# The same linear attention and PReLU layer, its list of operations written out in another order

## The chip, the cores and the metric

The kernel runs on one core of a Trainium2 chip. The metric is device microseconds (us) of one execution. The core has five engines with an instruction queue each: TensorE (PE; PEld is its weight loads), VectorE (DVE), ScalarE (ACT), GpSimd (POOL) and SyncE (SP), which does nothing here but issue transfers. Every queue runs strictly in the order in which the program was written; an instruction that waits holds up all behind it on its engine, and nothing on the others.

## The reference

q, k and v are 4 batches x 8 heads x 768 positions x 64 (float32). Attention is linear with a decay per head: within a block, products of q and k are multiplied by powers of the head's lambda and applied to v; across blocks, a 64 x 64 state per head is decayed and added to. Its output, as 3072 tokens x 512, goes through a two-layer network.

```python
intra = einsum('bhij,bhjd->bhid', einsum('bhic,bhjc->bhij', qb, kb) * Dmask, vb)
inter = einsum('bhid,bhde->bhie', qb * lam_pow, kv_state)
kv_state = lam_block * kv_state + einsum('bhsd,bhse->bhde', kb * rev_pow, vb)
h = x @ w_in                                  # 512 x 2048
out = (maximum(h, 0) + alpha * minimum(h, 0)) @ w_out   # 2048 x 512
```

## The kernel before, in words

The tokens are taken in six chunks of 512 (two batches x 256 positions). A chunk has four attention units, so there are 24, numbered 0 to 23: unit n belongs to chunk n // 4, to batch half (n // 2) % 2 and to head half n % 2. For a unit the program writes these steps:

- `load` brings float32 keys or queries (512 KB for a batch half, by SP's queue or, with ring=1, by POOL's, L89); `load16` brings queries of the first chunks, and all values, cast to half precision on the way by POOL's queue (L102).
- `cast` (L248 ACT, L250 DVE, L252 POOL) copies keys or queries into one half-precision tile qk. `turn` (L291) transposes that tile on PE for units 0 to 7, and `turned` copies the result from PSUM to qkT; from unit 8 on `turn_by_dma` (L305) has SP issue a transposing transfer instead.
- `key_decayed` (L279) and `decayed` (L321) multiply keys and turned queries by powers of lambda.
- `cluster(old, new)` on PE finishes unit old (L344 with the state RD, L374 with the masked scores) and starts unit new (scores s at L362, key-value products at L391).
- `masked` (L403, DVE) multiplies the scores by the decay mask; `state` (L428 DVE, L425 ACT) updates the state; `spread` copies it into RD, where the next cluster reads it; `out_of` copies the unit's output to xT.

The network: `up` (L457) makes 128 rows of h from w_in for a whole chunk or one batch half, in a PSUM bank; `below` (L468, ACT) takes the negative part m; `gate` (L481, DVE) joins them to g, which frees the bank for a later `up`; `down` (L491) and, for chunks 3 to 5, `product` (L598) multiply g by w_out. w_in and w_out come in four pieces each by POOL's queue (`load_win` L110, `load_wout` L116).

At the start `fill` (L238) keeps PE busy with products of the identity that nobody reads; `slopes` (L229, L230) transposes alpha on PE and has DVE make oma from it; `decay_mask`, `key_decay` and `query_decay` are exponentials on ACT; `causal` zeroes the masks; `hold` writes one element of a key tile on DVE, so that the tile's load waits for DVE to reach that place. `warm_up` sets one element on DVE and takes its logarithm on ACT (L179), for which ACT loads a table of functions.

The order of all this is a list of 887 calls at the end of the function. The call order is the queue order of each engine; semaphores do the rest. Nothing is planned at run time.

Of the kernel before, what the change touches and what calls it, by code (L numbers as in the profile page):

```python
# [11 lines left out]
def kernel(  # L12
# [434 lines left out]
    G = {}  # L447
# [213 lines left out]
    zeros(1, 1)  # L661
    identity()
    load("k", 0, 0, 0)
    load_alpha()
    zeros(2, 1, "G")
    zeros(0, 0)
    load("q", 0, 0, 0)
    hold("k", 0, 1, 0)
    load16("q", 0, 0, 1)
    load("k", 0, 0, 1)  # L670
    load16("v", 0, 0, 0)
    fill(6, 2)
    fill(36, 2)
    hold("k", 1, 0)
    logs()
    key_decay(0)
    zeros(1, 0)
    cast(0, "k", "V")
    key_decay(1)
    zeros(0, 1)  # L680
    decay_mask(3, 1)
    cast(0, "q", "G")
    fill(16, 2)
    turn(0)
    load16("q", 0, 1)
    hold("k", 2, 0)
    cast(1, "k", "V")
    key_decayed(0, "V")
    query_decay(1)
    load("k", 0, 1, 1)  # L690
    decay_mask(2, 1)
    decay_mask(0, 0)
    fill(15, 2)
    cast(3, "k", "V")
    load16("v", 0, 0, 1)
    decay_mask(1, 0)
    load16("v", 0, 1)
    query_decay(2)
    turned(0, "A")
    key_decayed(1, "V")  # L700
    query_decay(0)
    cast(1, "q", "V")
    key_decayed(3, "V")
    load("k", 0, 1, 0)
    fill(5, 2)
    decay_mask(1, 1)
    state_decay()
    decay_mask(0, 1)
    turn(1)
    decayed(0, "V")  # L710
    cluster(None, 0)
    causal(0, 1)
    turned(1, "A")
    load_win(0)
    query_decay(3)
    load16("q", 1, 0)
    zeros(3, 0)
    spread(0, 1, "A", True)
    causal(0, 0)
    load16("v", 1, 0)  # L720
    decayed(1, "G")
    cast(2, "k", "V")
    masked(0, 1)
    fill(17)
    masked(0, 0)
    cast(2, "q", "A")
    state(0, 0)
    decay_mask(2, 0)
    decay_mask(3, 0)
    causal(1, 1, "G")  # L730
    load("k", 1, 0)
    turn(2)
    cluster(0, 1, True)
    cast(3, "q", "A")
    state(0, 1)
    causal(1, 0, "G")
    turned(2, "V")
    load_win(1)
    masked(1, 1)
    turn(3)  # L740
    state(1, 0)
    spread(1, 1, "A", True)
    masked(1, 0)
    out_of(0, "V")
    cluster(1, None)
    turned(3, "A")
    out_of(1, "A")
    slopes(2)
    key_decayed(2, "G")
    cluster(None, 2)  # L750
    masked(2, 0)
    state(1, 1)
    decayed(2, "G")
    spread(2, 1, "A", True)
    cast(4, "k", "G")
    load16("q", 1, 1)
    masked(2, 1)
    spread(9, 0, "A")
    state(2, 0)
    up(0, 0, 0, 2)  # L760
    cast(4, "q", "G")
    cluster(2, 3, True)
    state(2, 1)
    below(0, 0, 0)
    load_win(2)
    spread(3, 1, "A", True)
    decayed(3, "G")
    key_decayed(4, "G")
    state(3, 0)
    turn(4)  # L770
    gate(0, 0, 0)
    masked(3, 1)
    cast(5, "k", "G")
    up(0, 2, 0, 2)
    out_of(2, "A")
    below(0, 2, 0)
    cast(5, "q", "A")
    masked(3, 0)
    zeros(3, 1)
    gate(0, 2, 0)  # L780
    turned(4, "A")
    fill(14, 0)
    cluster(3, None)
    state(3, 1)
    up(0, 1, 0, 0)
    up(0, 3, 0, 2)
    out_of(3, "V")
    below(0, 1, 0)
    below(0, 3, 0)
    up(0, 6, None, 1)  # L790
    load_win(3)
    cast(6, "q", "G")
    gate(0, 1, 0)
    below(0, 6, None)
    key_decayed(5, "G")
    up(0, 2, 1, 0)
    gate(0, 3, 0)
    below(0, 2, 1)
    up(0, 5, None, 2)
    zeros(2, 0)  # L800
    hold("k", 1, 1)
    cluster(None, 4)
    gate(0, 2, 1)
    below(0, 5, None)
    decayed(4, "G")
    gate(0, 6, None)
    up(0, 0, 1, 0)
    cast(7, "q", "G")
    below(0, 0, 1)
    load16("v", 1, 1)  # L810
    gate(0, 5, None)
    masked(4, 1)
    up(0, 4, None, 1)
    gate(0, 0, 1)
    load_wout(1)
    up(0, 8, None, 2)
    below(0, 4, None)
    up(0, 3, 1, 0)
    load("k", 1, 1)
    gate(0, 4, None)  # L820
    below(0, 8, None)
    state(4, 0)
    below(0, 3, 1)
    gate(0, 8, None)
    load_wout(0)
    gate(0, 3, 1)
    turn(5)
    masked(4, 0)
    up(0, 7, None, 1)
    spread(4, 1, "G")  # L830
    turned(5, "A")
    below(0, 7, None)
    state(4, 1)
    up(0, 1, 1, 2)
    below(0, 1, 1)
    cast(6, "k", "G")
    gate(0, 7, None)
    key_decayed(6, "G")
    gate(0, 1, 1)
    spread(10, 0, "A")  # L840
    up(0, 9, None, 0)
    cluster(4, 5)
    up(0, 11, None, 2)
    below(0, 9, None)
    load_wout(2)
    turn(6)
    state(5, 0)
    up(0, 14, None, 1)
    decayed(5, "G")
    spread(5, 1, "G")  # L850
    masked(5, 0)
    state(5, 1)
    load("k", 2, 0, ring=1)
    masked(5, 1)
    below(0, 11, None)
    cast(7, "k", "G")
    gate(0, 9, None)
    up(0, 12, None, 0)
    gate(0, 11, None)
    load("q", 2, 0, ring=1)  # L860
    below(0, 14, None)
    out_of(4, "A")
    hold("k", 3, 0)
    below(0, 12, None)
    up(0, 10, None, 2)
    turned(6, "V")
    below(0, 10, None)
    key_decayed(7, "G")
    gate(0, 14, None)
    load16("v", 2, 0)  # L870
    gate(0, 12, None)
    cluster(5, None)
    up(0, 15, None, 1)
    out_of(5, "A")
    up(1, 0, 0, 0)
    below(1, 0, 0)
    below(0, 15, None)
    gate(0, 10, None)
    hold("k", 2, 1)
    up(0, 13, None, 2)  # L880
    below(0, 13, None)
    cluster(None, 6)
    load_wout(3)
    gate(1, 0, 0)
    gate(0, 15, None)
    gate(0, 13, None)
    state(6, 0)
    up(1, 2, 0, 0)
    below(1, 2, 0)
    masked(6, 1)  # L890
    gate(1, 2, 0)
    decayed(6, "V")
    state(6, 1)
    turn(7)
    down(0, 2, 0, 1)
    turned(7, "V")
    up(1, 1, 0, 2)
    load("k", 2, 1, ring=1)
    spread(11, 0, "V")
    spread(6, 1, "G")  # L900
    down(0, 2, 1, 2)
    spread(14, 0, "V")
    cast(8, "k", "A")
    down(0, 1, 0, 0)
    down(0, 1, 1, 2)
    masked(6, 0)
    down(0, 2, 2, 2)
    below(1, 1, 0)
    gate(1, 1, 0)
    key_decayed(8, "V")  # L910
    key_decayed(9, "G")
    cast(9, "k", "A")
    cast(8, "q", "G")
    cluster(6, 7)
    down(0, 0, 0, 2)
    down(0, 0, 1, 1)
    state(7, 0)
    turn_by_dma(8)
    decayed(7, "V")
    down(0, 0, 2, 1)  # L920
    spread(8, 0, "G")
    spread(7, 1, "A")
    cast(10, "k", "A")
    masked(7, 1)
    decayed(8, "G")
    cast(9, "q", "V")
    down(0, 1, 2, 2)
    down(0, 2, 3, 2)
    masked(7, 0)
    state(7, 1)  # L930
    out_of(6, "V")
    down(0, 0, 3, 1)
    cast(11, "k", "V")
    store(0, 0)
    store(0, 2)
    cluster(7, 8)
    load("q", 3, 1)
    down(0, 1, 3, 2)
    spread(13, 0, "V")
    load("k", 3, 1, ring=1)  # L940
    out_of(7, "V")
    state(8, 0)
    load("q", 3, 0, ring=1)
    up(1, 3, 0, 2)
    up(1, 4, None, 1)
    spread(8, 1, "G")
    key_decayed(11, "G")
    masked(8, 1)
    store(0, 1)
    below(1, 3, 0)  # L950
    masked(8, 0)
    state(8, 1)
    gate(1, 3, 0)
    load16("v", 2, 1)
    turn_by_dma(9)
    up(1, 5, None, 0)
    cast(14, "k", "G")
    decayed(9, "G")
    cast(14, "q", "G")
    below(1, 4, None)  # L960
    key_decayed(10, "G")
    cluster(8, 9)
    gate(1, 4, None)
    below(1, 5, None)
    up(1, 0, 1, 2)
    below(1, 0, 1)
    load("q", 2, 1)
    gate(1, 5, None)
    up(1, 1, 1, 1)
    state(9, 0)  # L970
    gate(1, 0, 1)
    below(1, 1, 1)
# [603 lines left out]
```

## Time and profile before

| | us |
|---|---|
| median of 3 runs | 214.76 (214.64 to 214.83) |
| the profiled execution's own time | 216.86 |
| its span, first to last instruction | 214.80 |
| PE busy in the span | 199.9 (93%) |
| DVE, ACT, POOL busy | 163.7, 109.4, 100.9 |
| read from and written to HBM | 27.28 MB, 6.29 MB |

In a row of the timeline stand the start, the length, the engine (q: its sequencer issues a transfer), the line, operation, out<-in with shapes, how many, and in brackets the idle time of the engine before it and what ended that. Rows that follow closely are merged. In a row of the table of stretches stand the stretch, its length, busy time of the engines with instructions in brackets, the granted TensorE clock, the busy share of the DMA engines (it can exceed 1, since overlapping packets count apart) and GB/s. TensorE's granted clock is 0.999 over the span.

### The profile page before, as it was taken

How to read it: one execution, taken by the hardware profiler on the slowest of the kernel's cores; microseconds unless marked ns; L12 is line 12 of the kernel's file. 1: busy time of each engine (PE TensorE's matmuls, PEld its weight loads, DVE VectorE, ACT ScalarE, POOL GpSimd, SP SyncE). 2: the span in 40 equal slices, each digit the busy share in tenths (PEclk: the TensorE clock that was granted, in tenths of full speed). 3: DMA queues.
4: the chain of work that ended last, by engine and by line, in shares of the span. 5: the costliest groups of instructions: out<-in, count | busy, mean ns of one | idle time of the engine just before them, and what ended most of it. 6: DMA issues, size and time to landing. Idle time of an engine off the chain costs nothing.

```text
span 214.8 us, 5663 instructions
## 1 busy us (share of the span) xinstructions
PE 199.9 (93%) x2286; PEld 124.1 (58%) x2286; DVE 163.7 (76%) x335; ACT 109.4 (51%) x219; POOL 100.9 (47%) x149
## 2 busy tenths in 40 slices
PE   4967899999999779999999989999999999999992
PEld 4955565655645345546454535556667756866881
DVE  3888699895959995599977948979785669478721
ACT  3988676542645512546764565327546334344320
POOL 7879788951829994990299265331040000000000
PEclk9999999999999999999999999999999999999999
DMA  4999999999999999999764299649223120102213
GB/s 122 270 194 195 195 212 202 252 226 229 323 240 200 217 224 236 231 189 252 151 119 80 76 217 149 173 123 192 56 99 53 52 98 2 49 25 76 70 56 121
DMA packets 59754, 33.54 MB, mean 156 GB/s; under 512 B 34496, under 2 KB 55504, under 8 KB 59728
## 3 DMA queue, kind: packets, MB, share of 16 engines
q0 software_dynamic: 22528, 14.03, 42.6%
q1 hardware_dynamic: 35296, 16.00, 34.0%
q10 hardware_dynamic: 1904, 3.16, 4.2%
q8 instruction: 18, 0.29, 0.5%
q14 instruction: 8, 0.07, 0.1%
HBM read 27.28 MB, written 6.29 MB: 156 GB/s over the span
## 4 chain that ended last, share of the span: by engine, by line
PE 72%; DMA 13%; POOL 6%; DVE 3%; issue 3%; ACT 1%; SPq 0%; DVEq 0%; ACTq 0%
PE h_ps L457 32%; PE p_ps L598 17%; PE o_ps L491 15%; DMA qraw<-in_q_dram 8%; DMA qh<-in_q_dram 5%; PE s L362 3%; PE acc L374 2%; PE acc L344 2%; POOL vh L102 2%; POOL qk L252 1%; DVE g L481 1%; POOL qdT L321 1%; PE acc L391 1%; DVE RD L250 1%; POOL RD L252 1%
## 5 line engine op out<-in xcount | busy, mean ns | idle before, releaser
L457 PE MATMUL h_ps<-xT,w_in_sb 128*128 128x512 f16 (+1 forms) x416 | 92.2, 363 | 3.3 <-DVE g L481 2.7
L481 DVE SCALAR_TENSOR_TENSOR g<-m,oma,h_ps 128x512 f16<-128x512 f32 (+1 forms) x104 | 71.5, 704 | 24.5 <-ACT m L468 23.0
L468 ACT ACTIVATE m<-h_ps 128x512 f32<-128x512 f32 (+1 forms) x104 | 57.1, 564 | 53.3 <-PE h_ps L457 50.0
L457 PEld LDWEIGHTS <-w_in_sb 128*128 128x128 f16 x416 | 39.2, 98 | 40.5 <-issue 3.2
L491 PE MATMUL o_ps<-w_out_sb,g 128*128 128x512 f16 x192 | 45.4, 379 | 0.0
L403 DVE TENSOR_TENSOR sm<-s,dmask 128x512 f16<-128x512 f32 x48 | 32.2, 685 | 2.7 <-PE s L362 2.5
L491 PEld LDWEIGHTS <-g 128*128 128x128 f16 x192 | 18.3, 98 | 20.8
L321 POOL TENSOR_TENSOR qdT<-qkT,qdecay 128x512 f16<-128x512 f16 (+1 forms) x19 | 19.8, 1045 | 5.9 <-DMA qkT<-qk 5.3
L598 PEld LDWEIGHTS <-g 128*128 128x128 f16 x192 | 18.7, 98 | 4.1
L279 POOL TENSOR_TENSOR kdec<-kraw,kdecay 128x512 f16<-128x512 f32 x17 | 18.1, 1064 | 5.1 <-PE acc L391 3.5
L252 POOL COPY RD<-R 64x128 f16<-64x128 f16 x34 | 12.1, 357 | 10.3 <-DVE R L428 9.3
L598 PEld LDWEIGHTS <-gsum 128*128 128x128 f16 x144 | 14.0, 98 | 3.4
L428 DVE SCALAR_TENSOR_TENSOR R<-R,rdecay,acc 128x64 f16<-128x64 f16 x60 | 14.0, 275 | 1.7 <-ACT R L425 0.8
L622 ACT ACTIVATE o_sb<-p_ps 128x512 f32<-128x512 f32 (+1 forms) x16 | 7.7, 489 | 13.6 <-PE p_ps L598 12.2
L511 ACT ACTIVATE o_sb<-o_ps 128x512 f32<-128x512 f32 x12 | 7.2, 597 | 12.5 <-PE o_ps L491 11.9
L252 POOL CAST qk<-qraw 128x512 f16<-128x512 f32 x12 | 7.3, 613 | 10.9 <-DMA qraw<-in_q_dram 10.8
L598 PE MATMUL p_ps<-wsum,gsum 128*128 128x256 f16 x96 | 12.0, 273 | 0.0
L598 PE MATMUL p_ps<-w_out_sb,g 128*128 128x256 f16 x96 | 11.9, 272 | 0.0
L248 ACT ACTIVATE xT<-acc 128x512 f16<-128x512 f32 x14 | 8.3, 595 | 6.8 <-DVE R L428 5.2
L598 PE MATMUL p_ps<-wsum,g 128*128 128x256 f16 x96 | 11.8, 273 | 0.0
L102 POOL DMA_DIRECT2D vh<-in_v_dram x13 | 11.7, 901 | 0.0
L238 PE MATMUL op_fill<-ident 128*128 128x128 f16 x109 | 8.8, 245 | 2.9 <-POOL ident masks.py:199 2.7
(88 smaller groups left out, 214.2 us busy)
## 6 DMA issues: line engine op xcount, KB each, us to landing
kraw<-in_k_dram SPq DMA_DIRECT2D x6, 512.0 KB, 8.7
out_dram<-o_sb ACTq DMA_DIRECT2D x12, 256.0 KB, 6.0
out_dram<-o_sb SPq DMA_DIRECT2D x24, 128.0 KB, 1.9
vh<-in_v_dram POOLq DMA_DIRECT2D x11, 256.0 KB, 8.0
qraw<-in_q_dram SPq DMA_DIRECT2D x5, 512.0 KB, 7.0
w_in_sb<-in_moe_w_in_dram POOLq DMA_DIRECT2D x4, 512.0 KB, 8.1
w_out_sb<-in_moe_w_out_dram POOLq DMA_DIRECT2D x4, 512.0 KB, 8.5
kraw<-in_k_dram POOLq DMA_DIRECT2D x4, 512.0 KB, 8.3
```

Source lines behind the costliest of these rows:

```text
L102: nc.gpsimd.dma_start(out=rows16(x, c, bi)[:, ds(h0, n), :], in_=source({"q": q, "v": v}[x], c, bi, h0, n))
L238: nc.tensor.matmul(t[:, 0:128], lhsT=ident, rhs=ident, start=True, stop=True)
L252: nc.gpsimd.tensor_copy(out=out, in_=in_)
L279: engine(eng).tensor_tensor(out=kdec, in0=kr, in1=d.unsqueeze(3).to_broadcast([128, 2, 4, D]), op=ALU.mult)
L321: engine(eng).tensor_tensor(out=x, in0=y, in1=d.unsqueeze(2).to_broadcast([128, 4, n, 64]), op=ALU.mult)
L403: nc.vector.tensor_tensor(out=t["sm"][hl], in0=t["s"][hl], in1=mask_of(hl, units[n][2]), op=ALU.mult)
L428: nc.vector.scalar_tensor_tensor(out=then[:, hp], in0=R[b, hh, i][:, hp], scalar=rdecay[:, 2 * hh + hp : 2 * hh + hp + 1], in1=kv[:, hp], ...
L457: nc.tensor.matmul(h_ps[:, 0:n] if bi is None else h_ps[:, 0:n].rearrange("p (e j) -> p e j", e=2), lhsT=w_in_sb[:, gi, ts(f, 128)], rhs=x ...
L468: nc.scalar.activation(m[:, 0:n], HP[c, f, bi][:, 0:n], AF.Relu, scale=-1.0)
L481: nc.vector.scalar_tensor_tensor(out=g, in0=mv, scalar=oma[:, f : f + 1], in1=hv, op0=ALU.mult, op1=ALU.add)
L491: nc.tensor.matmul(O[c, t], lhsT=gated(c, f)[:, t // 2, t % 2, :], rhs=w_out_sb[:, f, :], start=(f == 0), stop=(f == NF - 1),)
L598: nc.tensor.matmul(acc, lhsT=lhsT, rhs=rhs, start=(first and j == 0), stop=(j == NJ - 1), skip_group_check=True,)
```

## The change

The 887 calls are written in another order, and 97 of them have another engine, transfer queue or PSUM bank. The number of calls of each kind, the fills' total of 109 among them, is the same, and PE's instructions are as many as before (4573). Nothing outside the list changes. Two lines of the difference:

```diff
-    load("k", 1, 0)
+    load("k", 1, 0, ring=1)
```

What stands where is better seen in the queues. The first place is POOL's queue at the start of the program, from the last copy of the identity on. qh and vh are queries and values in half precision, kraw and qraw keys and queries in float32; 4x128 is half a tile, 8x128 a whole one. Before:

```order
L161 CAST ident_142<-ident 16x16
L175 MEMSET RD_1_136 128x512
L102 DMA qh<-in_q_dram 128x4x128
L102 DMA vh<-in_v_dram 128x4x128
L252 CAST qk_240<-qraw 128x512
L102 DMA qh<-in_q_dram 128x8x128
L102 DMA vh<-in_v_dram 128x4x128
L102 DMA vh<-in_v_dram 128x8x128
L110 DMA w_in_sb<-in_moe_w_in_dram 128x4x512
L102 DMA qh<-in_q_dram 128x8x128
L102 DMA vh<-in_v_dram 128x8x128
```

And now:

```order
L161 CAST ident_142<-ident 16x16
L102 DMA qh<-in_q_dram 128x4x128
L89 DMA kraw<-in_k_dram 128x4x128
L102 DMA vh<-in_v_dram 128x4x128
L102 DMA vh<-in_v_dram 128x8x128
L102 DMA qh<-in_q_dram 128x8x128
L102 DMA vh<-in_v_dram 128x4x128
L89 DMA kraw<-in_k_dram 128x8x128
L110 DMA w_in_sb<-in_moe_w_in_dram 128x4x512
L279 TENSOR_TENSOR kdec<-kraw,kdecay 128x512
L102 DMA qh<-in_q_dram 128x8x128
```

Half of the first chunk's second keys and all of the second chunk's first keys (kraw 8x128) have come from SP's queue to POOL's, ahead of the first piece of w_in; the cast that waited for queries is gone from between the issues; a memset of RD now stands ahead of the identity instead of behind it.

The second place is DVE's and ACT's queues in the first chunk. On DVE, from the last copy of llp on, before:

```order
L192 COPY llp<-loglam 64x4
L175 MEMSET RD_0_133 128x256
L250 CAST qk_240<-kraw 128x512
L175 MEMSET RD_1_132 128x256
L85 MEMSET kraw 1x1
L250 CAST qk_276<-kraw 128x512
```

And now, with unit 0's tile called qk_234:

```order
L192 COPY llp<-loglam 64x4
L175 MEMSET RD_0_133 128x256
L250 CAST qk_234<-qraw 128x512
L230 TENSOR_SCALAR oma<-at_ps 128x16
L250 CAST qk_234<-kraw 128x512
L85 MEMSET kraw 1x1
```

oma, which stood far behind in the first chunk, now stands ahead of the cast of unit 0's keys; PE has 47 fills (36 + 5 + 6) ahead of the transpose that oma reads, and does that transpose before it turns unit 0. On ACT, from the first m on, now:

```order
L468 ACTIVATE m<-h_ps 128x256
L179 ACT_TABLE_LOAD
L179 ACTIVATE warm<-one 128x1
L425 ACTIVATE R_0_1_101<-acc 128x128
L248 ACTIVATE RD_1_134<-h_acc 64x2x64 x2
L425 ACTIVATE R_1_1_106<-h_acc 128x128
L248 ACTIVATE xT<-h_acc 128x4x64 x2
L468 ACTIVATE m<-h_ps 128x256
```

The table load and the logarithm of `warm_up` stood in the fourth chunk before, between two m. They now stand behind the first m and ahead of the state copies of units 2 and 3, unit 3's spread and unit 2's output copies.

The third place is chunk 2's transfers (units 8 to 11). On POOL, from `decayed(8)` on, now (before, this product was followed by loads of the fourth chunk's second keys and first queries):

```order
L321 TENSOR_TENSOR qdT<-qkT,qdecay 128x512
L102 DMA vh<-in_v_dram 128x8x128
L89 DMA qraw<-in_q_dram 128x8x128
L102 DMA vh<-in_v_dram 128x8x128
L89 DMA kraw<-in_k_dram 128x8x128
L252 CAST qk_1257<-qraw 128x512
L321 TENSOR_TENSOR qdT<-qkT,qdecay 128x512
```

On SP, from unit 8's transpose on, before:

```order
L305 DMA_TRANSPOSE qkT<-qk_1147 128x8x128
L89 DMA qraw<-in_q_dram 128x8x128
L305 DMA_TRANSPOSE qkT<-qk_1171 128x8x128
L89 DMA qraw<-in_q_dram 128x8x128
L305 DMA_TRANSPOSE qkT<-qk_1249 128x8x128
L89 DMA kraw<-in_k_dram 128x8x128
L305 DMA_TRANSPOSE qkT<-qk_1273 128x8x128
```

And now:

```order
L305 DMA_TRANSPOSE qkT<-qk_1233 128x8x128
L305 DMA_TRANSPOSE qkT<-qk_1143 128x8x128
L89 DMA qraw<-in_q_dram 128x8x128
L305 DMA_TRANSPOSE qkT<-qk_1255 128x8x128
L305 DMA_TRANSPOSE qkT<-qk_1257 128x8x128
L89 DMA qraw<-in_q_dram 128x8x128
L89 DMA kraw<-in_k_dram 128x8x128
```

The third chunk's second queries (for units 10 and 11) were SP's second qraw; they are now POOL's first qraw, behind a product that needs unit 8's transposed tile. The fourth chunk's first keys (kraw, for units 12 and 13) stood on SP ahead of unit 11's transpose; they now stand behind it and behind a load of queries. Further on the list differs in the same manner: who casts and copies, and what stands a few rows earlier or later. Three of the four pieces of w_out were issued ahead of the third chunk's first keys; now all four stand behind them.

More of the change, by code (lines that the diff above doesn't have):

```diff
@@ L697 @@
[L697 to L719, printed above, removed]
-    load16("v", 1, 0)
@@ L747 @@
[L747 to L755, printed above, removed]
-    load16("q", 1, 1)
[L757 to L765, printed above, removed]
+    load16("q", 0, 0, 1)
+    cast(0, "q", "V")
+    fill(5, 2)
+    fill(6, 2)
+    slopes(2)
+    load("k", 0, 1, 1, ring=1)
@@ L812 @@
+    gate(0, 0, 1)
+    masked(4, 0)
+    load("k", 1, 1)
+    below(0, 4, None)
+    load16("v", 1, 1)
+    up(0, 8, None, 2)
+    hold("k", 3, 0)
+    up(0, 3, 1, 0)
+    load_wout(0)
+    spread(4, 1, "A")
+    turn(5)
+    cast(6, "k", "G")
+    below(0, 3, 1)
+    below(0, 8, None)
+    gate(0, 4, None)
     masked(4, 1)
-    up(0, 4, None, 1)
-    gate(0, 0, 1)
+    gate(0, 3, 1)
+    turned(5, "A")
+    up(0, 7, None, 1)
     load_wout(1)
-    up(0, 8, None, 2)
-    below(0, 4, None)
-    up(0, 3, 1, 0)
@@ L838 @@
-    key_decayed(6, "G")
[L839 to L845, printed above, removed]
-    turn(6)
[L847 to L859, printed above, removed]
+    cluster(4, 5)
+    below(0, 9, None)
@@ L894 @@
[L894 to L913, printed above, removed]
-    cluster(6, 7)
-    down(0, 0, 0, 2)
+    down(0, 1, 1, 2)
```

1241 lines of the change are left out of this document (651 added, 590 removed).

## The prediction

> **What bounds the kernel now.** The page's busy times come first, with the DMA engines' share by fortieths of the span.
>
> ```profile
> PE 199.9 (93%) x2286; PEld 124.1 (58%) x2286; DVE 163.7 (76%) x335; ACT 109.4 (51%) x219; POOL 100.9 (47%) x149
> DMA  4999999999999999999764299649223120102213
> ```
>
> PE is busy for 93% of the span, and the change leaves its instructions as they are, so time can only come from PE's idle stretches and fills. The DMA engines are full from the second fortieth to the nineteenth, up to about 100 us: in that half a transfer that is issued later, or behind others, lands later. Next comes PE by stretches: the busy time, the granted clock and the DMA share.
>
> ```profile
> 0.00:24.00 24.00, 17.16 (x362) 1.00 1.28 195
> 68.00:80.00 12.00, 9.40 (x102) 1.00 1.26 233
> 103.00:108.00 5.00, 4.63 (x62) 1.00 0.75 188
> 125.00:131.00 6.00, 5.06 (x64) 1.00 0.99 170
> 131.00:211.00 80.00, 79.75 (x752) 1.00 0.34 88
> ```
>
> The clock is 1.00 throughout. From 131 us on PE loses a quarter of a microsecond in 80, so the last 80 us hold nothing to win, only something to lose. The losses lie in the head and in three short stretches. In the head, PE's timeline:
>
> ```profile
> 2.72 5.42 PE L238 MATMUL op_fill<-ident 128*128 128x128 f16 x58 [2.72 <-POOL ident masks.py:199]
> ...
> 18.48 0.61 PE L457 MATMUL h_ps<-xT,w_in_sb 128*128 128x256 f16 x4 [0.57 <-DMA w_in_sb<-in_moe_w_in_dram]
> ...
> 23.57 3.21 PE L457 MATMUL h_ps<-xT,w_in_sb 128*128 128x256 f16 x20
> ```
>
> Until 18.48 PE waits for keys, queries and attention's small copies; the first `up` then waits for w_in's first piece, and from 23.57 PE is full. The three short stretches are these, with the idle time in brackets:
>
> ```profile
> 75.56 0.60 PE L457 MATMUL h_ps<-xT,w_in_sb 128*128 128x256 f16 x4 [1.77 <-DVE g L481]
> ...
> 78.82 0.29 PE L344 MATMUL acc<-qdT,RD 128*128 128x128 f16 x2 [0.83 <-DVE RD L250]
> ```
>
> ```profile
> 107.09 0.29 PE L344 MATMUL acc<-qdT,RD 128*128 128x128 f16 x2 [0.37 <-POOL RD L252]
> ```
>
> ```profile
> 129.12 1.02 PE L457 MATMUL h_ps<-xT,w_in_sb 128*128 128x512 f16 x4 [0.94 <-DVE g L481]
> ```
>
> Together 1.77 + 0.83 + 0.37 + 0.94 = 3.9 us. Each has a cause that the new order touches. Behind 75.56 stands one copy on DVE, here between POOL's rows of the same time, and below them a copy of the same shape elsewhere:
>
> ```profile
> 72.21 1.18 POOL L321 TENSOR_TENSOR qdT<-qkT,qdecay 128x512 f16<-128x512 f16 x1
> 72.27 2.58 DVE L250 CAST qk<-kraw 128x512 f16<-128x512 f32 x1
> ```
>
> then POOL's next:
>
> ```profile
> 73.32 0.62 POOL L252 CAST qk<-qraw 128x512 f16<-128x512 f32 x1
> ```
>
> ```profile
> 48.29 0.41 DVE L250 CAST qk<-qraw 128x512 f16<-128x512 f32 x1
> ```
>
> The cast took 2.58 us instead of 0.41, while POOL went from one instruction to the next without a pause; the gate behind it on DVE, and PE behind that gate, lost most of the 2.17 us. The one at 129.12 is ACT's table load:
>
> ```profile
> 126.31 1.28 ACT L179 ACT_TABLE_LOAD   x1
> ```
>
> and the logarithm behind it:
>
> ```profile
> 127.60 0.20 ACT L179 ACTIVATE warm<-one 128x1 f32<-128x1 f32 x1
> ```
>
> That is 1.48 us between two m of a stretch in which PE's next bank hangs on them.
>
> **The change part by part.** *The keys in POOL's queue ahead of w_in: nothing.* The transfers ahead of w_in's first piece are the same set as before (SP's halves and the second chunk's first keys, POOL's queries and values), the DMA engines are full, and one set takes one time in either queue: I keep 18.4 us for its landing. The bounds are half a microsecond to either side. The cover is the backlog: the eight issues ahead of the kdec take some 0.9 us each and the transfers longer.
>
> *The head: +1.0.* oma now waits for 47 fills, ahead of the cast of unit 0's keys.
>
> ```profile
> 2.85 0.51 POOL L175 MEMSET RD<- 128x512 f16 x1
> ```
>
> ```profile
> 5.61 0.43 DVE L250 CAST qk<-kraw 128x512 f16<-128x512 f32 x1
> ```
>
> and next on DVE but for fills of memory:
>
> ```profile
> 6.99 0.82 DVE L250 CAST qk<-kraw 128x512 f16<-128x512 f32 x1 [0.68 <-DMA kraw<-in_k_dram]
> ```
>
> ```profile
> 10.00:15.00 5.00, 3.49 (x114) 2.88 (x112) 4.27 (x12) 4.31 (x12) 3.84 (x5) 1.00 1.66 208
> 15.00:20.00 5.00, 3.65 (x116) 2.84 (x115) 4.33 (x13) 4.08 (x13) 4.64 (x7) 1.00 1.58 191
> ```
>
> The identity is 0.51 us later, since a memset of this length moves ahead of it; 47 fills at 5.42 / 58 = 0.093 us take 4.4 us; so DVE, which has the first cast done at about 6.0, stands until 2.72 + 0.51 + 4.4 = 7.6, or 7.9 with the hand-over. That is 1.9 us of standing in place of 0.68. DVE is then busy for 8.60 of the 10 us from 10 to 20 (third busy time in the rows), so 1.4 us of pauses can take up some of the 1.2 us; but PE's clusters run in turn with DVE's masks, and little of a pause that waits for PE can be used. On ACT, 1.28 + 0.20 = 1.48 us now stand ahead of unit 2's output copies, whose bank a fill and the next `up` need; ACT has 8.39 of 10 us filled there. The two delays overlap. The head costs nothing if the pauses take up all, and 1.2 + 1.48 = 2.7 us if none: I take 1.0, near the single delays.
>
> *The second chunk's second keys: +0.3.* POOL's cast of them stands ahead of two pieces of w_out.
>
> ```profile
> 32.81 0.61 POOL L252 CAST qk<-kraw 128x512 f16<-128x512 f32 x1 [1.30 <-DMA kraw<-in_k_dram]
> ```
>
> ```profile
> 25.88 0.37 SPq L89 DMA_DIRECT2D kraw<-in_k_dram  x1
> ```
>
> SP issued them at 25.88 and they landed at 32.8, 6.9 us later. Their `hold` now stands behind the gate of the seventh `up`, some 2 us later, so I put the landing at 34.9; behind it POOL has the cast, an issue, a product and two copies (0.61 for the cast by the row, some 2 us for the rest, an estimate from it) before unit 5 can end at 37.5, just when PE comes there. That is a tie, so I take 0.3, between 0 and 1.2.
>
> *Unit 8's transpose: +0.4; unit 10's: +0.6.*
>
> ```profile
> 52.75 1.17 POOL L321 TENSOR_TENSOR qdT<-qkT,qdecay 128x512 f16<-128x512 f16 x1 [5.26 <-DMA qkT<-qk]
> ```
>
> ```profile
> 46.46 1.35 SPq L305 DMA_TRANSPOSE qkT<-qk  x1
> ```
>
> and behind it on SP:
>
> ```profile
> 52.49 0.58 SPq L89 DMA_DIRECT2D qraw<-in_q_dram  x1
> 60.21 1.24 SPq L305 DMA_TRANSPOSE qkT<-qk  x1
> ```
>
> ```profile
> 59.56 0.63 ACT L248 ACTIVATE qk<-qraw 128x512 f16<-128x512 f32 x1 [0.67 <-DMA qraw<-in_q_dram]
> ```
>
> ```profile
> 67.30 0.42 PE L362 MATMUL s<-qkT 64*64 64x128 f16 x16
> ```
>
> Unit 8's transpose goes at 46.46 and has landed at 52.7, when PE's scores want it. It now waits for two casts on DVE behind a gate and a key product, which I put at 49: 2.5 later, against a PE that comes 1.3 later by the terms above and one `down` (0.86) later by its own order: 0.3 to 0.4 is left. For units 10 and 11, the queries leave SP's queue (issued at 52.49, cast at 59.56, turned tile asked for at 67.30 with no slack that a wait shows) for POOL's, behind the product at 52.75 (1.17) and a load of values (0.9). Measured from unit 8's landing that is an issue 2.2 us later; against it stand one `up` (0.86) that now comes ahead of unit 9's end, and the 0.4 already waited. About 1 us is left, less what a shorter backlog in POOL's queue gives: 0.6, between 0 and 2.5.
>
> *Unit 12's transpose: +1.1.*
>
> ```profile
> kraw<-in_k_dram SPq DMA_DIRECT2D x6, 512.0 KB, 8.7
> ```
>
> and for the transposes, with the median us to the landing last in both:
>
> ```profile
> qkT<-qk SPq DMA_TRANSPOSE x16, 6.2
> ```
>
> ```profile
> 84.38 0.42 PE L362 MATMUL s<-qkT 64*64 64x128 f16 x16
> ```
>
> The fourth chunk's first keys stood on SP right behind unit 10's transpose. Now they follow unit 11's and a load. With unit 10's going at 64.2, SP gets to them at about 69; 7.5 us for the load (the row's median is 8.7), a cast and 6.2 for the transpose make 83.8. PE wants it at 84.38 before; less 0.86 for its order, less the 2.7 us of stops ahead of that which I take out, plus 2.3 of the terms above, 83.1. With half a microsecond for DVE's queue, 1.1 is left; between 0 and 3.
>
> *The three stops: -3.9, of which 1.3 come back.* The table load is gone from its place, and the 0.94 with it; other copies and casts meet there now. But DVE has as many copies as before in the middle, and POOL still works on end, so I give a third of the 3.9 back: between none and all.
>
> The sum is +1.0 + 0.3 + 0.4 + 0.6 + 1.1 - 3.9 + 1.3 = +0.8. The profiled span is 214.80, its execution 216.86 and the median of the runs 214.76; nothing at either end of the span changes, so the sum goes on the median: 215.5 us.
>
> **The rivals.** *Collisions decide.* Unit 12's keys now release a DVE cast and a POOL product (behind which POOL has four copies) at once. If POOL is first, DVE stands as at 72.27, for 2.2 us, and unit 12's transpose with it; POOL's long standing for those keys speaks for it, DVE's coming later than they land against it. That gives 215.5 + 2.2 = 217.7. [...]
>
> *The transfers come in time.* If POOL's shorter compute queue lets loads go earlier and the transposes of units 8, 10 and 12 are there when PE is, their 0.4 + 0.6 + 1.1 = 2.1 us go, and the time is 213.4; with the 1.3 of returns gone too, 212.1. The transposes' spread of several microseconds between issue and landing leaves room; the full DMA half speaks against it. The point from which it decides is unit 10's queries landing by 62.5.
>
> *It does nothing that counts.* The head takes up the delays and PE's small stops fall elsewhere by as much: 214.8.
>
> **How the numbers follow.** 0.2% is 0.43 us, about what a measurement of this kernel can tell from no change. The forecast (215.5, with the values from 214.9 to 216.7) gets 0.42, collisions 0.17, transfers in time 0.27, nothing 0.14. Faster is 0.27, the same 0.14, slower 0.42 + 0.17 = 0.59. The range reaches from 212.8, midway between the two times of the transfers in time, to 218.5, collisions with half of the 1.7 that the head may cost beyond my 1.0.
>
> **What would show it.** In the new profile: DVE's oma ends at 7.6 to 8.3 with a pause ahead of it of near 2 us; the seventh `up`, for a whole chunk, starts at 25 to 26, against some 24.5 (23.57 plus two half ups); ACT's table load stands near 20 us and 129 us has no stop; the scores of units 10 and 12 wait for SP's transposes. Wrong would be a PE that is full by 24 us, a stop beyond 131 us, or w_in's first piece landing outside 18 to 19 us.

## The result, and the profile after

The changed kernel takes 223.11 us (median of four runs, 219.63 to 224.06) against 214.80 for the kernel before: a ratio of 1.026, with a 95% interval from 1.021 to 1.031. Run again later, it took 222.24 against 215.58, a ratio of 1.0284 (1.0238 to 1.0330). The ratios here and below leave out runs in a slower state, and the medians do not, so the two need not agree. By the ratios the kernel is slower by some 6 us, where I had forecast 0.8 and a range up to 218.5.

The profiled execution of the changed kernel is its shortest run: own time 219.63, span 217.6. Its busy times and granted clock by fortieths:

```profile
PE 201.7 (93%) x2286; PEld 125.6 (58%) x2286; DVE 169.8 (78%) x342; ACT 113.9 (52%) x230; POOL 90.3 (41%) x132
PEclk9889999999999999999999999999999999999999
```

POOL has 10.6 us less work than before and DVE 6.1 more, part of it because some of DVE's instructions take longer (a copy 1.13 us in place of 0.28, below). PE has as many instructions as before, yet is busy for 1.8 us more, out of the 2.8 by which the span is longer. In the second and third fortieth the clock is below full, which it never was in the profile before. PE in the head; the first row is unit 0's turn, and the last holds a half `up` and, right behind it, the first `up` for a whole chunk:

```profile
9.57 1.03 PE L291 MATMUL tp<-ident,qk 128*128 128x128 f16 x8 [1.45 <-DVE kraw L85]
...
17.71 0.40 PE L291 MATMUL tp<-ident,qk 128*128 128x128 f16 x4 [1.80 <-DVE qk L250]
...
27.63 1.47 PE L457 MATMUL h_ps<-xT,w_in_sb 128*128 128x256 f16 x8
```

Before, that whole `up` came right behind the two half ups that begin at 23.57, at some 24.5. A half `up` holds PE for 0.43 us, so it now begins at some 28.1, 3.6 us later. In both long waits PE waits for DVE (the 1.45 and the 1.80). DVE in the same time:

```profile
8.16 0.17 DVE L230 TENSOR_SCALAR oma<-at_ps 128x16 f32<-128x16 f32 x1 [2.03 <-PE at_ps L229]
8.25 1.26 DVE L250 CAST qk<-kraw 128x512 f16<-128x512 f32 x1
...
10.52 1.13 DVE L250 COPY qk<-qh 128x512 f16<-128x512 f16 x1
...
12.99 1.49 DVE L279 TENSOR_TENSOR kdec<-kraw,kdecay 128x512 f16<-128x512 f32 x1
```

oma comes when I said, at 8.33, after a pause of 2.03. What I did not have is what follows: DVE has no pause of more than 0.2 us from there to 25 us, and its instructions are stretched. The copy at 10.52 takes 1.13 us, against 0.28 for the quickest of its shape in this profile; the product at 12.99 takes 1.49 against 0.68 at 9.91. POOL beside them:

```profile
9.95 1.54 POOL L279 TENSOR_TENSOR kdec<-kraw,kdecay 128x512 f16<-128x512 f32 x1
...
12.87 1.06 POOL L207 TENSOR_TENSOR dmask<-dmask,keep 128x384 f32<-128x384 f32 x1
```

The first is unit 2's key product, which now stands right behind w_in's first piece; the second is a product with the mask. The cast at 8.25, 1.26 us in place of 0.41, has only POOL's issues beside it, and the rows do not show what stretched it. Behind the head, the stops at 75.56, 78.82, 107.09 and 129.12 are gone, and others stand elsewhere, these three and one of 0.30 at 52.48:

```profile
58.95 0.42 PE L362 MATMUL s<-qkT 64*64 64x128 f16 x16 [0.97 <-DVE sm L403]
```

```profile
94.94 1.02 PE L457 MATMUL h_ps<-xT,w_in_sb 128*128 128x512 f16 x4 [0.93 <-DVE g L481]
106.11 0.40 PE L344 MATMUL acc<-qdT,RD 128*128 128x128 f16 x4 [0.48 <-DVE xT L250]
```

None of them waits for a transposing transfer. Unit 12's scores start at 86.18 with no idle time that the view prints.

### The profile page after: what moved, and what is told of

It is laid out like the page before. It is cut to its first block, busy times and chain, and to the rows that moved or that the text cites. A ratio compares the mean times of both kernels' runs of the same rounds, so it can differ in the third digit from the quotient of the medians.

```text
span 217.6 us, 5652 instructions
## 1 busy us (share of the span) xinstructions
PE 201.7 (93%) x2286; PEld 125.6 (58%) x2286; DVE 169.8 (78%) x342; ACT 113.9 (52%) x230; POOL 90.3 (41%) x132
## 4 chain that ended last, share of the span: by engine, by line
PE 75%; DVE 15%; DMA 3%; issue 2%; ACT 2%; POOL 1%; ACTq 0%; DVEq 0%; POOLq 0%
PE h_ps L457 35%; PE p_ps L598 17%; PE o_ps L491 13%; PE s L362 3%; DMA qkT<-qk 3%; DVE sm L403 3%; DVE g L481 2%; PE op_fill L238 2%; PE acc L374 2%; DVE kdec L279 2%; PE acc L344 2%; DVE R L428 1%; DVE qk L250 1%; DVE RD L250 1%; PE acc L391 1%
## 5 line engine op out<-in xcount | busy, mean ns | idle before, releaser
L491 PEld LDWEIGHTS <-g 128*128 128x128 f16 x192 | 18.4, 98 | 20.8
L321 POOL TENSOR_TENSOR qdT<-qkT,qdecay 128x512 f16<-128x512 f16 (+1 forms) x17 | 19.2, 1128 | 24.5 <-DMA qkT<-qk 11.7
L252 POOL COPY RD<-R 64x128 f16<-64x128 f16 x30 | 9.4, 312 | 21.7 <-DVE R L428 15.2
L279 POOL TENSOR_TENSOR kdec<-kraw,kdecay 128x512 f16<-128x512 f32 x14 | 15.5, 1105 | 2.4 <-DMA kraw<-in_k_dram 2.1
L238 PE MATMUL op_fill<-ident 128*128 128x128 f16 x109 | 9.4, 256 | 4.0 <-POOL ident masks.py:199 3.3
L362 PE MATMUL s<-qkT 64*64 64x128 f16 x384 | 10.3, 222 | 1.4 <-DVE sm L403 1.2
L238 PEld LDWEIGHTS <-ident 128*128 128x128 f16 x109 | 8.5, 118 | 4.6 <-POOL ident masks.py:199 3.2
```

The source lines that it names most:

```text
L238: nc.tensor.matmul(t[:, 0:128], lhsT=ident, rhs=ident, start=True, stop=True)
L279: engine(eng).tensor_tensor(out=kdec, in0=kr, in1=d.unsqueeze(3).to_broadcast([128, 2, 4, D]), op=ALU.mult)
L321: engine(eng).tensor_tensor(out=x, in0=y, in1=d.unsqueeze(2).to_broadcast([128, 4, n, 64]), op=ALU.mult)
L362: nc.tensor.matmul(s[hl][ds(a * 64, 64), hp, 1 - e, :].rearrange("p (e j) -> p e j", e=2), lhsT=t["qkT"][p, 1, e, hp, ds(a * 64, 64)], rhs ...
L491: nc.tensor.matmul(O[c, t], lhsT=gated(c, f)[:, t // 2, t % 2, :], rhs=w_out_sb[:, f, :], start=(f == 0), stop=(f == NF - 1),)
```

## The experiments

Ratios are to the kernel before, run beside each version on the same chip, with 95% intervals; 1% is 2.15 us.

**The changed kernel again.** No edit.

> The changed kernel itself once more, beside the others of this call. Its four runs went from 219.63 to 224.06 us with clocks from 0.992 to 0.985, while the kernel before keeps to 214.6 to 216.0. Theory A (the head is where it loses: PE stands from 8.1 to 9.6 us and the granted clock is 0.87, 0.50 and 0.78 in the two-microsecond stretches from 8 to 14 us; how long the low clock lasts differs from run to run): 219 to 224, and the longer runs have the lower clock. Theory B (the spread comes from transfers in the middle): 219 to 224 with clocks that don't go with the times.

Measured: 222.24 us (220.76 to 225.38), ratio 1.0284 (1.0238 to 1.0330). The clock does not order these runs: one of 220.93 had 0.974 and one of 222.33 had 0.992. So Theory A's second half is not borne out here; where the spread comes from is taken up below.

**Head of before, rest of after.**

```diff
-    load("q", 0, 0, 0)
...
-    gate(0, 1, 0)
+    zeros(1, 1)
...
+    below(0, 3, 0)
     up(0, 6, None, 1)
```

> Head of the kernel before (all calls up to the first up for a whole chunk, 132 of them, warm_up at its old place), then the changed kernel's order. By the traces the changed kernel has lost 4.5 us more of PE's time than the kernel before at 30 us, and 2.8 more at the end. Theory A (the head carries the loss and the rest gains): 214.8 - 1.7 = 213.1, between 212.5 and 214.5, and no spread. Theory B (the rest carries it): 217 to 222.

Measured: 223.03 us, ratio 1.0372 (1.0319 to 1.0426), with runs from 219.62 to 224.65: as slow as the changed kernel (1.0238 to 1.0330) or slower, and by the median above both theories. DVE and PE in its profile just behind the seam:

```profile
24.65 2.36 DVE L250 COPY RD<-R 64x128 f16<-64x128 f16 x2
27.04 0.87 DVE L481 SCALAR_TENSOR_TENSOR g<-m,oma,h_ps 128x256 f16<-128x256 f32 x2
```

```profile
27.58 1.88 PE L457 MATMUL h_ps<-xT,w_in_sb 128*128 128x256 f16 x8 [2.02 <-DVE g L481]
```

Two copies that take 0.39 together elsewhere took 2.36 beside two products of POOL and an issue between them, with the gate and PE's next `up` behind them. The run is no clean test of the rest: joining two orders made a wait that neither had. It is mended in a later run. It also says something on the clock. Its head is that of the kernel before, and yet:

```profile
18.00:20.00 2.00, 1.37 (x17) 0.56 1.74 186
20.00:22.00 2.00, 2.00 (x59) 0.59 1.30 205
```

Behind PE's busy time stands the granted clock, 0.56 and 0.59, where the kernel before had 1.00. One head can show the drop or not. In the changed kernel's first profile the clock was 0.87, 0.50 and 0.78 in the two-microsecond stretches from 8 to 14 us. What lowers it no run shows.

**slopes alone back.**

```diff
-    slopes(2)
     load("k", 0, 1, 1, ring=1)
...
+    slopes(2)
     cluster(None, 2)
```

> The changed kernel with slopes alone (oma) back at its old place, behind unit 1's end, so that DVE casts unit 0's keys without waiting for 47 fills. Theory A1 (oma's wait is the cause in the head: DVE stands 2.03 us, PE then 1.5, and the granted clock falls to 0.50): the low clock is gone, the clock of the span is 0.998 or more, and the time is 2.5 to 4.5 under the changed kernel's of the same call, 216 to 219. Theory A2 (the loads' order and DVE's and POOL's collisions in the head are the cause, oma only lies beside them): within 1 us of the changed kernel, with its spread.

Measured: 220.62 us, ratio 1.0208 (1.0154 to 1.0261), 1.6 us under the changed kernel run beside it, with intervals that overlap a little. That is between the two theories, and the traces do not settle it: the row that holds the first whole `up` begins at 27.67 in this run's profile, against 27.63 and 29.02 in the changed kernel's two. So what oma's wait costs in the new head stays open, and the low clock (0.980 to 0.992) stays.

**Fills ahead.**

```diff
+    fill(16, 2)
     turn(0)
     load("k", 1, 0, ring=1)
-    fill(16, 2)
```

> The changed kernel with the 16 fills that stand behind unit 0's turn put ahead of it, so that PE has work while DVE casts unit 0's keys: the wait for the cast stays, PE's idle time in it goes. Theory A1a (PE's idle time is what lowers the clock): clock 0.998 or more and the half-speed stretch near 10 us is gone, time 1 to 3 under the changed kernel's of the same call. Theory A1b (the wait itself costs, the clock is a small part): within 0.7 us of the changed kernel.

Measured: 220.52 us, ratio 1.0247 (1.0201 to 1.0293). The interval holds the changed kernel's 1.0284, so this is not told from no change. Its profile says why the clock can't be judged by it:

```profile
8.00:10.00 2.00, 1.63 (x26) 1.00 1.60 178
...
18.00:20.00 2.00, 2.00 (x55) 0.50 1.12 160
20.00:22.00 2.00, 2.00 (x46) 0.50 1.45 192
```

The 0.50 of 10 to 12 us in the changed kernel's first profile is gone (1.00 there now) and stands at 18 to 22 instead, behind another wait for DVE (PE is busy for 0.00 of the 2 us from 16 to 18). But in the second profile of the unedited kernel it stands there too (0.83 from 16 to 18 us, 0.50 from 18 to 24), so the edit need not have moved it. In this run the times do go with the clock: 219.77 and 220.02 us at 1.000 and 0.999, 222.63 at 0.980. A share of the clock in the spread is not ruled out.

**Head of after, rest of before.**

```diff
-    zeros(1, 1)
...
-    below(0, 3, 0)
+    load("q", 0, 0, 0)
...
+    gate(0, 1, 0)
     up(0, 6, None, 1)
```

> The changed kernel's head (134 calls, up to the first up for a whole chunk), then the order of the kernel before. Theory A (the head costs what the trace shows at 30 us, 4.5 us of PE's time, and the old rest does not take it back): 4.5 above the kernel before, between 3.5 and 6. Theory B (the new rest is what costs, and the head's delay is taken up by later waits): within 1.5 us of the kernel before. Theory D (seams between two orders cost by themselves, as in the run with the head of before): 6 or more above.

Measured: 219.68 us, ratio 1.0201 (1.0170 to 1.0232), 4.3 us above the kernel before. Theory A holds (3.5 to 6): the old rest does not take the head's loss back.

**slopes and the key product back.**

```diff
-    key_decayed(2, "G")
     key_decayed(1, "V")
...
+    slopes(2)
+    key_decayed(2, "G")
     cluster(None, 2)
```

> The changed kernel with slopes at its old place and POOL's key product of unit 2 moved back to just ahead of unit 2's start. Theory C (DVE bounds the head, and POOL's early products lengthen DVE's copies beside them: in the changed kernel the copies and products at 8.25, 10.52 and 12.99 us took 1.26, 1.13 and 1.49 us in place of 0.42, 0.28 and 0.68, 2.5 us together): DVE's excess there falls by at least 1 us, PE turns units 2 and 3 some 1 to 2 us sooner, and the time is 1 to 2 under the run with slopes alone moved back (220.6). Theory A2' (the loads' order bounds the head): within 0.7 of 220.6.

Measured: 217.85 us, ratio 1.0092 (1.0042 to 1.0142): 1.2%, or 2.5 us, under the run with slopes alone back, more than expected. The two edits together take the ratio from 1.0284 to 1.0092, some 4 of the 6 us. DVE in the two runs, from unit 0's key product to the copy of unit 1's turned tile (qkT<-tp), some rows left out. First with slopes alone back:

```profile
8.43 1.54 DVE L279 TENSOR_TENSOR kdec<-kraw,kdecay 128x512 f16<-128x512 f32 x1
...
10.64 1.01 DVE L279 TENSOR_TENSOR kdec<-kraw,kdecay 128x512 f16<-128x512 f32 x1
11.58 1.21 DVE L321 TENSOR_TENSOR qdT<-qkT,qdecay 128x256 f16<-128x256 f16 x1
12.71 1.48 DVE L279 TENSOR_TENSOR kdec<-kraw,kdecay 128x512 f16<-128x512 f32 x1
14.12 0.68 DVE L250 COPY qkT<-tp 128x1024 f16<-128x1024 f16 x1
```

Then with the product back too:

```profile
8.48 0.69 DVE L279 TENSOR_TENSOR kdec<-kraw,kdecay 128x512 f16<-128x512 f32 x1
...
10.07 0.62 DVE L279 TENSOR_TENSOR kdec<-kraw,kdecay 128x512 f16<-128x512 f32 x1
10.62 0.41 DVE L321 TENSOR_TENSOR qdT<-qkT,qdecay 128x256 f16<-128x256 f16 x1
10.95 0.68 DVE L279 TENSOR_TENSOR kdec<-kraw,kdecay 128x512 f16<-128x512 f32 x1
11.55 0.68 DVE L250 COPY qkT<-tp 128x1024 f16<-128x1024 f16 x1
```

POOL's two products in the first of these runs:

```profile
9.95 1.14 POOL L279 TENSOR_TENSOR kdec<-kraw,kdecay 128x512 f16<-128x512 f32 x1
...
12.44 1.20 POOL L207 TENSOR_TENSOR dmask<-dmask,keep 128x384 f32<-128x384 f32 x1
```

The same four DVE instructions take 5.24 us in the one run and 2.40 in the other, 2.84 less, and the copy that PE waits for comes 14.12 - 11.55 = 2.57 sooner. DVE has no pause from 8 to 18 us in the first run, so the moved product costs through DVE, and not by a transfer. Not all of the 2.84 lies beside the moved product itself: the DVE product at 10.64 does, the one at 12.71 lies beside the mask product, which the moved one held up (it starts at 11.29 without it), and the one at 8.43 ends as POOL's product begins, so that what stretched it is not shown. Here, then, DVE's products with two inputs, and not only its copies, took longer beside POOL's products: 1.01 and 1.48 us at 10.64 and 12.71, in place of 0.62 and 0.68. Even so the head is not wholly back: the row that holds the first whole `up` begins at 25.75, which puts that `up` at some 26.2, 1.7 us behind that of the kernel before.

**slopes early in the kernel before.**

```diff
+    slopes(2)
     cast(0, "k", "V")
...
-    slopes(2)
     key_decayed(2, "G")
```

> The kernel before with slopes alone moved early, ahead of the cast of unit 0's keys, behind 42 fills. Theory A1 (oma's wait by itself costs the head some 1.5 us and lets the clock drop): 1 to 3 above the kernel before. Theory A2 (the wait is taken up by pauses, as my 1.0 for all of the head had it): within 1.0 of the kernel before.

Measured: 215.44 us, ratio 0.9996 (0.9968 to 1.0024). In the old head, where DVE has pauses, the wait for oma costs nothing (A2); it was 1.56 us there, behind 42 fills. In the new head, where DVE has none, undoing it gave 0.8%, which the intervals do not tell from nothing.

**The head of before, mended.** Against the run with the head of before:

```diff
     up(0, 6, None, 1)
+    load_win(3)
+    hold("k", 1, 1)
+    load("k", 1, 1)
...
-    load_win(3)
-    spread(8, 0, "V")
...
     down(0, 0, 2, 1)
+    spread(8, 0, "G")
```

> The run with the head of before, with four calls of the seam put where the kernel before has them: the last piece of w_in and the second chunk's second keys with their hold right behind the head, and unit 8's spread on POOL, later. In that run PE lost 6.5 us more than in the kernel before from 25 to 45 us: 2.2 at 27.58 behind a DVE copy of RD that took 1.82 in place of 0.19 us beside POOL's issue and product, about 1 by the half clock behind it, and some 2.5 at 40 to 43 us by keys that landed at 39.5 in place of 32.7. Theory E (these three are its loss, and the rest of the changed order is better than the old one by the three stops): 211.5 to 214. Theory B (the changed rest costs in other places too): 216 or more.

Measured: 218.60 us, ratio 1.0115 (1.0065 to 1.0164). Theory B: without the head's loss, and with the old stops gone, the changed rest still costs 2.5 us. With the head's 4.3 this makes 6.8, against 6.1 for the changed kernel in its second set of runs.

**Ten spreads on ACT** (the edit is the same for all ten).

```diff
-    spread(20, 1, "V")
+    spread(20, 1, "A")
```

> The changed kernel with its ten spreads on DVE given to ACT. Theory F (behind the head the changed order puts DVE copies of R to RD beside POOL's products, where one takes up to 1.97 us more than its 0.4 for two, by chance of which comes first, and the gate behind it comes late): 1 to 3.5 us under the changed kernel, ratio to the kernel before 1.012 to 1.024 in place of 1.028, and the stops at 103 to 106 and 145 to 153 us gone. Rival G (these copies hide behind PE's work, and ACT's m come later instead): 1.026 or more.

Measured: 222.03 us, ratio 1.0305 (1.0251 to 1.0358): nothing gained. In its profile PE waits for ACT's copy of the state at 62 us instead. Given for all ten spreads at once, Theory F is not borne out.

**Without the table load, in both kernels.**

```diff
-    warm_up()
```

> The changed kernel without warm_up, so without the second load of the logarithm's table and a logarithm that nobody reads. Theory H (the table load in the head delays unit 2's output copies, and the next fills and ups, by some 1.3 us): 0.7 to 1.5 under the changed kernel, ratio 1.021 to 1.025. Rival (ACT's delay lies beside DVE's, which ends later anyway): within 0.5 us, ratio 1.026 to 1.031.

> The kernel before without warm_up in the same way. Its table load stands at 126.31, with a stop of PE of 0.94 at 129.12 behind it. Theory H: 0.9 under the kernel before, ratio 0.9945 to 0.9965. Rival (the stop comes from the gates' order, not from the table): 0.998 to 1.002.

Measured: the changed kernel 222.21 us, ratio 1.0278 (1.0223 to 1.0334), so no cost of the table load is seen in its head, though the interval would hide 1 us; the kernel before 214.61 us, ratio 0.9940 (0.9910 to 0.9970), so at 126 us it costs 1.3.

**The three stops of before.**

```diff
-    cast(15, "k", "V")
+    cast(15, "k", "A")
...
-    cast(13, "q", "V")
+    cast(13, "q", "A")
...
-    spread(10, 1, "V")
+    spread(10, 1, "A")
...
-    warm_up()
```

> The kernel before without warm_up and with three DVE copies given to ACT: unit 15's keys (2.58 us in place of 0.41 at 72.27), unit 13's queries and unit 10's spread of the state (1.83 in place of 0.18 at 76.94). Theory F (DVE's copies beside POOL's work make these stops): the stops of 1.77, 0.83 and 0.94 are gone, and nothing takes their place: 3.0 to 3.7 under the kernel before, ratio 0.983 to 0.986. Rival (PE is then held by the next late thing, as a third of the 3.9 in my sum): 0.987 to 0.992.

Measured: 213.45 us (212.81 to 214.53), ratio 0.9915 (0.9887 to 0.9943). This version beats both kernels. PE by stretches:

```profile
68.00:80.00 12.00, 12.00 (x148) 1.00 1.28 239
125.00:131.00 6.00, 6.00 (x69) 1.00 1.08 173
```

The stops are gone entirely, 12.00 of 12 and 6.00 of 6 in place of 9.40 and 5.06. Yet the timed runs fell by 1.8 us and not by 3.5; 1.3 of it is the table load's (the run without it), which leaves some 0.5 for the two stops near 77 us that the profile shows at 2.60. The stretched cast at 72.27 is not in every execution. Five profiles have the old order there: the cast took 2.58 in the kernel before and 2.46 with the old order up to unit 16 (a run below), but 0.42, 0.92 and 0.65 with slopes early, without the table load and with two late spreads (the last run but one). Two of the five:

```profile
72.19 2.46 DVE L250 CAST qk<-kraw 128x512 f16<-128x512 f32 x1
```

```profile
72.31 0.42 DVE L250 CAST qk<-kraw 128x512 f16<-128x512 f32 x1
```

The profiled execution of the kernel before, whose own time, 216.86, is 2.1 above its median, is one that has the stop in full; by these profiles not every timed run does.

**Old engines in the new order.** One of the 67 and of the 82 calls:

```diff
-    cast(12, "k", "V")
+    cast(12, "k", "A")
```

> The mended run with the head of before (ratio 1.0115), its order kept, but each cast, product, spread and output copy from unit 6 on given to the engine that the kernel before gives it (67 calls). Theory K (the engines are the cause: more DVE copies beside POOL's products, each lengthened by chance): ratio 0.996 to 1.003. Rival L (order and transfers are the cause): 1.007 to 1.02, as without it.

> The changed order as it is, head included, with the engines of before for all casts, products, spreads and output copies (82 calls). Theory K: the rest's 1% goes and part of the head's, ratio 1.010 to 1.020. Rival L: 1.024 or more.

Measured: 225.24 us, ratio 1.0458 (1.0420 to 1.0495), and 228.35 us, ratio 1.0612 (1.0572 to 1.0652). Theory K falls: the new order wants its own engines. L is borne out only so far that the engines by themselves are not the cause.

**Change over at unit 16, both ways** (the part ahead of `cluster(15, 16)` from one order, the part behind it from the other).

```diff
     cluster(15, 16)
-    spread(19, 1, "V")
+    spread(19, 1, "A")
...
-    spread(22, 0)
+    spread(22, 0, "V")
```

> The order of before up to the cluster that starts unit 16 (519 calls), then the changed order, warm_up at its old place. From 135 us on the profiles of the changed order lost 4.1 to 7.3 us, those of the old order 3.3 to 3.9. Theory M (the loss lies behind unit 16): ratio 1.006 to 1.015. Rival N (ahead of it): 0.997 to 1.003.

> The mended run up to the cluster that starts unit 16, then the order of before. Theory M (the loss lies behind unit 16): ratio 0.994 to 1.002, since the old order's stops at 75 to 79 us are not in it. Rival N (ahead of it): 1.006 to 1.015.

Measured: old order first, 217.82 us, ratio 1.0125 (1.0081 to 1.0168); new order first, 222.48 us, ratio 1.0291 (1.0241 to 1.0341). The first says that the new order loses behind unit 16. The second is outside both theories, slower than either of the two that it joins, as the first seam was, with four stops of 0.7 to 1.3 us from 102 to 114 us, and tells nothing on that. POOL's busy time from 131 to 157 us, before and after:

```profile
131.00:157.00 26.00, 5.42 (x6) 1.00 0.60 136
```

```profile
131.00:157.00 26.00, 11.06 (x12) 1.00 0.69 156
```

The old order has POOL only issue and add there; the new one puts products there. In the run with the old order up to unit 16, DVE, POOL and PE:

```profile
142.58 1.27 DVE L250 COPY RD<-R 64x128 f16<-64x128 f16 x2
...
146.33 2.32 DVE L250 COPY RD<-R 64x128 f16<-64x128 f16 x2
148.67 0.75 DVE L481 SCALAR_TENSOR_TENSOR g<-m,oma,h_ps 128x512 f16<-128x512 f32 x1
```

```profile
145.91 1.48 POOL L321 TENSOR_TENSOR qdT<-qkT,qdecay 128x512 f16<-128x512 f16 x1
147.03 1.36 POOL L279 TENSOR_TENSOR kdec<-kraw,kdecay 128x512 f16<-128x512 f32 x1
```

```profile
146.47 1.02 PE L457 MATMUL h_ps<-xT,w_in_sb 128*128 128x512 f16 x4 [0.59 <-DVE g L481]
...
149.47 1.02 PE L457 MATMUL h_ps<-xT,w_in_sb 128*128 128x512 f16 x4 [1.06 <-DVE g L481]
```

Two copies that take 0.39 undisturbed stand from 146.33 until both of POOL's products are over (the first of them alone takes 2.12); the gate comes at 148.67, and PE stands for 1.06. In the profiled execution of the changed kernel the same copies took 0.39, at 149.58 with POOL's product at 150.46: there DVE came first.

```profile
149.58 0.39 DVE L250 COPY RD<-R 64x128 f16<-64x128 f16 x2
```

```profile
150.46 1.48 POOL L321 TENSOR_TENSOR qdT<-qkT,qdecay 128x512 f16<-128x512 f16 x1
```

**Two late spreads on ACT.**

```diff
-    spread(20, 1, "V")
+    spread(20, 1, "A")
...
-    spread(22, 0, "V")
+    spread(22, 0, "A")
```

> The order of before up to unit 16 and the changed order from there (ratio 1.0125), with two late spreads (of units 20 and 22, two copies each) given from DVE to ACT. Theory P (these copies wait for POOL's products beside them, and the gates and PE behind them: 1.27 and 2.32 us at 142.58 and 146.33, stops of 0.75 and 1.22): about 2 us less, ratio 1.002 to 1.006. Rival (ACT's queue or the next DVE copy beside POOL takes their place): 1.009 or more.

Measured: 215.53 us, ratio 1.0009 (0.9983 to 1.0035), 2.3 us under the run without the edit. Theory P holds: in this joined order, two pairs of copies of 0.4 us made the whole loss of the new order behind unit 16. PE in its profile goes on at the place of the 1.06 with no idle time that the view prints:

```profile
147.26 1.04 PE L457 MATMUL h_ps<-xT,w_in_sb 128*128 128x512 f16 x4
```

**slopes, product and the two spreads undone in the changed kernel** (the edits above together).

> The changed kernel with slopes and unit 2's key product back at their old places (ratio 1.0092) and the same two late spreads on ACT. If slopes, product and late copies are the whole of the slowdown: 1.000 to 1.004. If the late copies are not among its causes: 1.007 or more.

Measured: 217.69 us, ratio 1.0092 (1.0058 to 1.0127), the same as without the spreads. So in the changed order as a whole the late copies are not what holds it, or something takes their place. Its profiled execution has a span of 213.9, under the 214.8 of the kernel before, while most of its timed runs lie between 217 and 219: the profile does not show what a typical run loses. The last 0.9% stays open: what the new order loses behind the head has a shown cause only where the old order stands ahead of unit 16.

## Why the prediction was wrong, step by step

*What bounds the kernel*: right in the main. PE's instructions are as before, and the difference is PE's waiting and, in the head, its time at a lower clock (0.50 from 10 to 12 us). I also wrote that the last 80 us hold only something to lose, and then priced nothing there; with the old order up to unit 16, the new one lost 1.25% there, which two spreads gave back. This is the second step that failed: my terms behind the head add up to 2.4 - 3.9 + 1.3 = -0.2, and with the old head the new rest cost +2.5 (1.0115).

*The keys ahead of w_in: nothing*: right. The first piece of w_in landed at 18.58, against my 18.4, and nothing waited for it: the first `up` came at 21.83.

*The head: +1.0* is the step that failed. Measured by the head alone it is 4.3 us (1.0201), outside my bound of 2.7. oma's end and pause were as I said. The failure is in the sentence that followed: I took DVE's slack, "busy for 8.60 of the 10 us", from the old order, and let it hide the wait. In the new order that slack is filled (DVE has no pause from 8.2 to 18 us), and POOL's early key product, for which my sum had no term, lengthened DVE's work there: moving it alone back gave 2.5 us (1.0208 to 1.0092). oma's own wait costs nothing in the old head; in the new one undoing it gave 0.8%, with intervals that overlap. ACT's table load, on which I put as much weight, shows no cost there.

*Unit 5's, 8's, 10's and 12's keys and queries, +2.4 together*: not seen in the changed kernel, where none of PE's stops waits for a transfer. A likely reason, which no run shows by itself, is that PE came 3.6 us late out of the head and the transfers had that much longer. With PE early (the mended run, in a profiled execution of 221.16 us, 2.6 above its median) some appear:

```profile
37.82 0.28 PE L344 MATMUL acc<-qdT,RD 128*128 128x128 f16 x2 [1.30 <-POOL RD L252]
```

That is the end of unit 5, behind POOL's cast of its keys and the copies that follow: 1.30, against my 0.3 and a bound of 1.2. At 70.04 PE waits 0.25 for a transposed tile. The rival "the transfers come in time" was right for the changed kernel, for a reason that I had not named. (In unit 12's sum the stops taken out are 1.77 + 0.83 = 2.60, not 2.7; it changes little.)

*The three stops: -3.9, 1.3 of it back*: mis-sized. The two largest and the table load's, undone in the old order, give 1.8 us and not 3.5, since one of them is not in every execution. "DVE has as many copies as before in the middle" holds by the count (28 copies and casts before and 26 now from 35 to 131 us), but hides what changed: there, casts of keys and queries went from 5 to 10 and copies of the state from 18 to 10. DVE's casts and state copies over the whole program before, by shape and source:

```profile
L250 DVE COPY RD<-R 64x128 f16<-64x128 f16 x24 | 7.1, 297 | 0.2
L250 DVE CAST qk<-kraw 128x512 f16<-128x512 f32 x7 | 5.6, 804 | 2.3 <-DMA kraw<-in_k_dram 2.3
...
L250 DVE CAST qk<-qraw 128x512 f16<-128x512 f32 x2 | 0.8, 411 | 0.0
```

and now:

```profile
L250 DVE COPY RD<-R 64x128 f16<-64x128 f16 x20 | 6.5, 326 | 1.0 <-ACT R L425 0.8
...
L250 DVE CAST qk<-kraw 128x512 f16<-128x512 f32 x9 | 4.9, 556 | 0.0
...
L250 DVE CAST qk<-qraw 128x512 f16<-128x512 f32 x6 | 2.5, 426 | 0.0
L250 DVE COPY qk<-qh 128x512 f16<-128x512 f16 x4 | 2.4, 593 | 0.0
```

With one copy from qh before, that is 10 casts against 19, and 24 state copies against 20; the order lists showed both before any run.

*The rival "collisions decide"* was right that DVE can be held up beside POOL's products, at other places than its own (unit 12's cast): in the head (1.48 us in place of 0.68) and late (2.32 in place of 0.39), by products that POOL did not have there before: moving one product in the head gave 2.5 us, and moving two pairs of late copies in the joined order 2.3, each as much as the 2.2 that it priced for one meeting. Since such a meeting went one way at 146.33 (POOL's product 0.42 us ahead, 2.32 for the copies) and the other at 149.58 (0.88 behind, 0.39), it is also what I hold for the spread of the changed kernel's runs (219.63 to 225.38). No run shows that by itself, and the clock is not ruled out beside it; but the run without the old stops also has the narrowest runs of the experiments (212.81 to 214.53).

## What to carry to other kernels

When an order moves work between engines, list for each stretch what stands on DVE beside what on POOL in the new order: two short DVE copies beside POOL's products took 2.32 us here in place of 0.39, a two-input product 1.48 in place of 0.68, and slack read from the old order may not be there any more. Compare the profiled execution's own time with the median before crediting a stop that it shows; one that comes from a chance meeting may not be in the timed runs. And joining the halves of two tuned orders is a poor test until the seam's own waits are found in the trace and taken out.

## What the runs showed of the hardware that I had not expected

A DVE copy beside two POOL products that follow each other stood until both were over, not one: from 146.33 one copy took 2.12 us, and the next, behind them, 0.19, with the products at 145.91 (1.48) and 147.03 (1.36). And the granted clock fell in one of two kernels with the same head (0.56 and 0.59 against 1.00 and 1.00 from 18 to 20 and 20 to 22 us, with PE busy for 1.37 and 1.52 of the first 2). What that is worth stays open: the mean clock did not order the times of the changed kernel run again, and did order those with the fills ahead.
